# Sending the last 64 tokens of two batches in one transfer from interleaved partitions, and spreading the small row transfers that share the queue

## The chip, the cores and the metric

The kernel runs on one core of one Trainium2 chip. The metric is the time of one execution on the device in microseconds (us). Profiles are single executions; their span leaves out about 2 us of the time (427.3 us of span in the profiled run of the kernel before, 429.12 us of time).

## The reference

Sliding-window attention over 8 batches, 8 heads, 576 tokens and 64 channels per head feeds a spectral mixing layer:

```python
x = attention(q, k, v)                       # (8, 576, 512), window of 64 tokens
X = np.fft.rfft(x, axis=1)                   # 64 lowest modes are mixed
Y[:, :64] = complex einsum('bmd,mde->bme', X[:, :64], w_r + 1j * w_i)
y = np.fft.irfft(Y, n=576, axis=1)
u = x + y
return u + np.maximum(u @ w_ch, 0.0)         # (8, 576, 512) float32
```

The 64 pairs of 512x512 matrices w_r and w_i are most of the data read. What matters here is the end: u and the rectified product are formed tile by tile, and 9.44 MB of output leave the core.

## The kernel before

576 tokens are four tiles of 128 and a rest of 64. The rests of two batches share one tile, the *pair tile*: batch b on partitions 0 to 63, batch b+1 on 64 to 127. A whole-token tile pair (t, t+1) leaves as one transfer of 512 KB, 4 KB per partition; the pair tile leaves as two transfers of 64 partitions, 2 KB each. All of them are issued by SyncE. So are six small transfers, `send`, that copy eight late rows of a batch's spectrum (32 KB) to the tile that the matmuls of that batch read.

```python
def send(b):
    r0 = 2 * R + RL * (b - 2)
    nc.sync.dma_start(out=batch_tile(b)[128 - RL:].bitcast(FP32), in_=yl[r0:r0 + RL].bitcast(FP32))

def finish(n):
    b, t = seq[n]
    add(n, "Yb", True)                       # matmuls into PSUM
    ...
    nc.vector.tensor_tensor(out=ot[:, j], in0=ps, in1=x_sb[:, b, t, :], op=ALU.add)
    if t == NT - 1:                          # pair tile
        for i, queue in enumerate((nc.sync, nc.sync)):
            queue.dma_start(out=out[b + i, 128 * t:, :], in_=ot[64 * i:64 * i + 64, 0])
    ...
    elif j:                                  # two whole tiles
        nc.sync.dma_start(out=out[b, 128 * t - 128:128 * t + 128, :].rearrange("(p j) e -> p j e", j=2), in_=ot)

turn_of = {1: 3, 3: 4, 5: 5, 7: 6, 8: 7}     # after tile 1 send the rows of batch 3, ...
for n in range(NQ):                          # NQ = 36 tiles
    finish(n)
    if n in turn_of:                         # send(2), the first of the six, stands before this loop
        send(turn_of[n])
    ...                                      # rectify(n + 3), lay(n + 5)
```

The softmax here doesn't subtract the row's maximum and nothing guards it: scores larger than these inputs give would overflow.

Of the kernel before, what the change touches and what calls it, by code (L numbers as in the profile page):

```python
# [9 lines left out]
FP32 = mybir.dt.float32  # L10
FP32R = mybir.dt.float32r
BF16 = mybir.dt.bfloat16
# [14 lines left out]
def kernel(  # L27
# [10 lines left out]
    nc = tc.nc  # L38
    B, H, S, D = q.shape
# [532 lines left out]
    with ExitStack() as p2a:  # L572
# [4 lines left out]
        def channel(i):  # L577
            b, t = tiles[i]
            n = 1 if t == NT - 1 else 2
            psts = []  # L580
            for k in range(n):
                pst = ps_t.tile([128, NC, 128], BF16, name="pxt")
                for c in range(NC):
                    nc.tensor.transpose(out=pst[:, c, :], in_=x_sb[:, b, t + k, 128 * c:128 * c + 128],  # L584
                                        identity=ident_bf)
                psts.append(pst)
            for j in range(n):
                xT = xtp.tile([128, NC, 128], FP32R, name="xT")
                for k in range(n):
                    w = 128 // n  # L590
                    nc.vector.tensor_copy(out=xT[:, :, w * k:w * k + w], in_=view(psts[k], j, [[128, NC], [n, w]]))  # L591
                psz = ps_z.tile([128, DM], FP32, name="psz")
                for c in range(NC):
                    nc.tensor.matmul(out=psz, lhsT=xT[:, c, :], rhs=wch[:, c, :],  # L594
                                     start=(c == 0), stop=(c == NC - 1))
                nc.scalar.copy(out=channel_out(i + j), in_=psz)  # L596
            return n
# [3 lines left out]
        for m in range(L0 * MG):  # L601
# [13 lines left out]
            if m == Z_M - 2:  # L615

                with tc.tile_pool(name="tmpi", bufs=1, reuse_waits="tile") as tmp:
                    pcol = tmp.tile([128, 1], FP32, name="pcol")
                    nc.gpsimd.iota(pcol, pattern=[[0, 1]], base=0, channel_multiplier=1,
                                   allow_small_or_imprecise_dtypes=True)  # L620

                    SW = 128
                    pos = tmp.tile([128, SW + 64], FP32, name="pos")
                    nc.gpsimd.iota(pos[:, 0:SW], pattern=[[2, SW]], base=0, channel_multiplier=0,
                                   allow_small_or_imprecise_dtypes=True)
                    nc.gpsimd.iota(pos[:, SW:], pattern=[[1, 64]], base=512, channel_multiplier=0,
                                   allow_small_or_imprecise_dtypes=True)

                    def col(name):
                        return tmp.tile([128, 1], FP32, name=name)  # L630

                    def floor(d, p, name):
                        f = col(name)
                        nc.vector.tensor_scalar(out=f, in0=p, scalar1=1.0 / d, scalar2=0.5 / d - 0.5,
                                                op0=ALU.mult, op1=ALU.add)
                        nc.vector.tensor_scalar(out=f, in0=f, scalar1=MAGIC, scalar2=-MAGIC,
                                                op0=ALU.add, op1=ALU.add)
                        return f


                    for tab, row in ((trigI, pcol),):
                        fa, fb = floor(2 * MG, row, "fa"), floor(MG, row, "fb")

                        gcol, mcol = col("gcol"), col("mcol")
                        nc.vector.scalar_tensor_tensor(out=gcol, in0=fa, scalar=-2.0, in1=fb,
                                                       op0=ALU.mult, op1=ALU.add)
                        nc.vector.tensor_tensor(out=mcol, in0=fa, in1=fb, op=ALU.subtract)
                        nc.vector.scalar_tensor_tensor(out=mcol, in0=mcol, scalar=float(MG), in1=row,
                                                       op0=ALU.mult, op1=ALU.add)
                        for at, dg, dm in ((112 + ML, 1.0, -float(ML)), (112 + MG, -1.0, float(MG)),  # L650
                                           (112 + 2 * ML, -1.0, 0.0), (112 + 2 * ML + NLM, 1.0, -float(NLM))):
                            step = col("step")
                            nc.vector.tensor_single_scalar(out=step, in_=row, scalar=at - 0.5, op=ALU.is_ge)
                            nc.vector.scalar_tensor_tensor(out=gcol, in0=step, scalar=dg, in1=gcol,
                                                           op0=ALU.mult, op1=ALU.add)
                            if dm:
                                nc.vector.scalar_tensor_tensor(out=mcol, in0=step, scalar=dm, in1=mcol,
                                                               op0=ALU.mult, op1=ALU.add)
                        coef, coefs, coefc = col("coef"), col("coefs"), col("coefc")
                        nc.vector.tensor_single_scalar(out=coef, in_=mcol, scalar=0.0, op=ALU.is_equal)  # L660
                        nc.vector.tensor_scalar(out=coef, in0=coef, scalar1=-1.0 / S, scalar2=2.0 / S,
                                                op0=ALU.mult, op1=ALU.add)
                        nc.vector.tensor_tensor(out=coefs, in0=gcol, in1=coef, op=ALU.mult)
                        nc.vector.tensor_tensor(out=coefc, in0=coef, in1=coefs, op=ALU.subtract)
                        for i in range(NT):
                            n = SW if i < NT - 1 else 64
                            mt2 = tmp.tile([128, 2, SW], FP32, name="mti")[:, :, 0:n]
                            mt = mt2[:, 0, :]
                            nc.vector.tensor_scalar(out=mt, in0=pos[:, 0:SW] if n == SW else pos[:, SW:],
                                                    scalar1=float(256 * (i // 2) + i % 2) if n == SW else 0.0,  # L670
                                                    scalar2=mcol, op0=ALU.add, op1=ALU.mult)
                            tis = tmp.tile([128, SW], FP32, name="tis")[:, 0:n]
                            gen_trig(tmp, mt2, n, mt, tis, "i")
                            nc.vector.tensor_scalar(out=tis, in0=tis, scalar1=coefs, scalar2=None, op0=ALU.mult)
                            o = SW * i if n == SW else 576
                            nc.vector.scalar_tensor_tensor(out=tab[:, o:o + n], in0=mt, scalar=coefc, in1=tis,
                                                           op0=ALU.mult, op1=ALU.add)
                    nc.vector.tensor_scalar(out=view(trigI, 512, [[128, 2], [1, 64]]),
                                            in0=view(trigI, 0, [[64, 2], [1, 64]]), scalar1=0.0,
                                            scalar2=None, op0=ALU.mult)  # L680
                    nc.vector.tensor_scalar(out=view(YTl, R - RL, [[R, NC * B], [1, RL]]),
                                            in0=view(trigI, 0, [[RL, NC * B], [1, RL]]), scalar1=0.0,
                                            scalar2=None, op0=ALU.mult)
# [90 lines left out]
        for j in range(2):  # L774
            evac(x_sb[:, b, 2 * h + j, :], ps[j], j)

    spreads = [(b, h) for b in range(B) for h in range(2)]

    with tc.manual_schedule(engines={mybir.EngineType.PE}):
        for m in range(M0, ME):  # L780
            while len(spreads) > 2 * B * (ME - 1 - m) // (ME - M0):
                spread(*spreads.pop(0))
            if (m - M0) % 2 == 0 and (m - M0) // 2 < B // 2:
                b0 = m - M0
                mode(m, lambda: spectrum(b0))
# [48 lines left out]
    with tc.manual_schedule(engines={mybir.EngineType.PE, mybir.EngineType.Activation, mybir.EngineType.DVE,  # L834
# [20 lines left out]
        def add(n, what, stop):  # L855
            b, t = seq[n]
            for bb, r0, k in parts_of(b, t):
                tr = 128 * t + (64 - r0 if t == NT - 1 else 0)
                nc.tensor.matmul(out=tps[n], lhsT=trigI[:, tr:tr + 128], rhs=pair_tile(what, bb),  # L859
                                 start=False, stop=stop and r0 + k == 128, skip_group_check=True)  # L860

# [6 lines left out]
        def finish(n):  # L868
# [12 lines left out]
                return  # L881
            nc.vector.tensor_tensor(out=ot[:, j], in0=ps, in1=x_sb[:, b, t, :], op=ALU.add)  # L882
            if t == NT - 1:
                for i, queue in enumerate((nc.sync, nc.sync)):
                    queue.dma_start(out=out[b + i, 128 * t:, :], in_=ot[64 * i:64 * i + 64, 0])
            elif n == NQ - 2:
                nc.sync.dma_start(out=out[b, 128 * t:128 * t + 256, :].rearrange("(p j) e -> p j e", j=2)[:, 0],
                                  in_=ot[:, 0])
# [7 lines left out]
            if n == 2:  # L896
                nc.scalar.copy(out=yl[0:NR, 0], in_=psw[0:NR])
        send(2)
        turn_of = {1: 3, 3: 4, 5: 5, 7: 6, 8: 7}
        for n in range(NQ):  # L900
            finish(n)
            if n in turn_of:
# [39 lines left out]
```

## Time and profile before

| | |
|---|---|
| time, median of the first 3 runs | 429.73 us (429.59 to 430.24) |
| span of the profile | 427.3 us |
| weights stream, until the last weight matmul | 391.2 us |
| first DVE cast of the tail (it takes up the last weights' products) / last output add ends | 391.87 / 420.39 us |
| output leaves | 399 to about 426.1 us |

Three more lines say how the tail works. The first is from the page (busy time, share of the span, instructions of each engine), the others from the table of waits between 391 and 428 us (who waited for what: us in total, times, longest).

```profile
PE 322.1 (75%) x5179; PEld 230.8 (54%) x5186; DVE 176.1 (41%) x372; ACT 164.1 (38%) x290; POOL 89.4 (21%) x171
...
PEld pso L859 <- ACT pso L864: 1.7, 6, 0.4
DVE ot L882 <- PE pso L859: 1.1, 5, 0.3
```

The shares are averages over stages with different limits and say nothing of the tail. The waits do: in some 28 us of tail, PE's loads wait 1.7 us for ACT and DVE 1.1 us for PE. (A pair of names like `PEld pso L859 <- ACT pso L864` reads: the loads of line 859 waited for ScalarE's line 864.) The producers run at their pace, and what is left to win lies between the last add and the end.

### The profile page before, as it was taken

To read this page: it belongs to the slowest core of one execution; us is meant where nothing else is said; L and a number is where in the kernel's file an instruction comes from. 1 tells how busy PE (TensorE), PEld (TensorE's weight loads), DVE (VectorE), ACT (ScalarE), POOL (GpSimd) and SP (SyncE) were. 2 spreads that over 40 slices of the span, in tenths; PEclk is the share of its full clock that TensorE was granted. 3 is DMA by queue.
4 is the path that set the end of the run, shared out by engine and by line. 5 is a ranking of instruction groups with operands and counts; after the bars stand their busy time and mean duration, and the time that the engine had idled before them with its cause. 6 is when DMAs were issued, how large, how long until landed. Compare 5 with 4: busy or idle time off the path is not lost.

```text
span 427.3 us, 11629 instructions
## 1 busy us (share of the span) xinstructions
PE 322.1 (75%) x5179; PEld 230.8 (54%) x5186; DVE 176.1 (41%) x372; ACT 164.1 (38%) x290; POOL 89.4 (21%) x171
## 2 busy tenths in 40 slices
PE   6989998998998866422488877876367685498992
PEld 5755765765665566411367666654245452266781
DVE  5566765765764200306223332221113332141993
ACT  4585765866863221001022322222012221131991
POOL 7231231241112232211221221221111122100000
PEclk9999998999996655555588998899556965589997
DMA  7999999999999999999999999999999999993698
GB/s 142 212 213 213 213 212 213 214 211 214 214 213 213 214 213 261 214 214 213 213 213 215 213 212 214 214 214 213 212 215 213 214 213 214 214 214 68 219 351 333
DMA packets 28721, 92.16 MB, mean 216 GB/s; under 512 B 2896, under 2 KB 3152, under 8 KB 28672
## 3 DMA queue, kind: packets, MB, share of 16 engines
q0 software_dynamic: 25344, 81.80, 96.1%
q1 hardware_dynamic: 3184, 9.50, 6.0%
q8 instruction: 40, 0.66, 0.6%
q10 hardware_dynamic: 144, 0.13, 0.1%
q14 instruction: 9, 0.07, 0.0%
HBM read 162.53 MB, written 9.44 MB: 402 GB/s over the span
## 4 chain that ended last, share of the span: by engine, by line
DMA 51%; PE 32%; DVE 8%; issue 4%; ACT 2%; POOL 1%; DVEq 0%; POOLq 0%
DMA wt<-in_moe_w_i_dram 45%; PE pso L316 7%; PE pst L218 6%; DMA wy<-in_moe_w_i_dram 4%; PE pso L859 4%; PE psv L235 3%; DVE x_sb L324 3%; PE pss L372 3%; PE pss L272 2%; DMA wt<-in_moe_w_r_dram 2%; PE psx L338 2%; PE pss L291 2%; DVE vT L59 2%; PE psw L709 1%; DVE ot L882 1%
## 5 line engine op out<-in xcount | busy, mean ns | idle before, releaser
L563 PE MATMUL psy<-XQ,wt 128*128 128x16 bf16 x1616 | 61.4, 191 | 72.8 <-DMA wt<-in_moe_w_i_dram 37.6
L563 PEld LDWEIGHTS <-wt 128*128 128x128 bf16 x1616 | 53.2, 103 | 87.5 <-DMA wt<-in_moe_w_i_dram 42.4
L591 DVE CAST xT<-pxt 128x256 fp32r<-128x256 bf16 (+1 forms) x68 | 26.1, 434 | 61.8 <-PE pxt L584 39.4
L115 POOL DMA_DIRECT2D wt<-in_moe_w_r_dram x54 | 29.0, 537 | 87.8 <-DMA wt<-in_moe_w_r_dram 42.2
L596 ACT CAST Z<-psz 128x512 fp32r<-128x512 f32 x36 | 21.1, 586 | 66.9 <-PE psz L594 66.6
L115 POOL DMA_DIRECT2D wt<-in_moe_w_i_dram x52 | 27.9, 536 | 84.7 <-DMA wt<-in_moe_w_i_dram 53.7
L594 PE MATMUL psz<-wch,xT 128*128 128x512 f32 x144 | 45.3, 457 | 0.0
L297 ACT ACTIVATE et<-pss 128x512 bf16<-128x512 f32 x72 | 39.2, 599 | 13.2 <-PE pss L291 13.2
L316 PE MATMUL pso<-vt,et 128*64 128x65 bf16 (+1 forms) x576 | 34.3, 210 | 5.2 <-DVE x_sb L324 5.1
L316 PEld LDWEIGHTS <-et 128*64 128x64 bf16 (+1 forms) x576 | 23.9, 114 | 17.3 <-issue 9.8
L594 PEld LDWEIGHTS psz<-wch,xT 128*128 128x128 f32 x144 | 29.2, 217 | 5.8 <-ACT Z L596 0.4
L324 DVE TENSOR_TENSOR x_sb<-pso,rcp 128x640 bf16<-128x640 f32 x32 | 26.3, 822 | 0.9
L859 PE MATMUL pso<-Y,trigI 128*128 128x512 f32 x80 | 23.1, 402 | 0.1
L59 DVE CAST YT<-psy 128x256 fp32r<-128x256 f32 x6 | 2.5, 423 | 49.4 <-PE psy L563 49.4
L882 DVE TENSOR_TENSOR ot<-pso,x_sb 128x512 f32<-128x512 f32 x35 | 22.2, 685 | 1.5 <-PE pso L859 1.1
L59 DVE CAST x_sb<-psj 128x512 bf16<-128x512 f32 x16 | 11.0, 688 | 27.2 <-PE psj L771 27.1
L58 ACT CAST YT<-psy 128x256 fp32r<-128x256 f32 x6 | 2.2, 373 | 50.7 <-DVE YT L59 50.7
L272 PE MATMUL pss<-band,ident_bf 64*64 64x512 bf16 x136 | 20.5, 414 | 1.5 <-ACT et L297 1.5
L59 DVE COPY vT<-pst 128x768 bf16<-128x768 bf16 x16 | 15.3, 957 | 13.0 <-PE pst L218 13.0
L58 ACT CAST x_sb<-psj 128x512 bf16<-128x512 f32 x16 | 9.4, 586 | 26.9 <-PE psj L771 26.9
L864 ACT ACTIVATE pso<-pso 128x512 f32<-128x512 f32 x36 | 19.1, 597 | 0.0
L859 PEld LDWEIGHTS pso<-Y,trigI 128*128 128x128 f32 x80 | 14.5, 188 | 5.5 <-ACT pso L864 1.7
(158 smaller groups left out, 496.3 us busy)
## 6 DMA issues: line engine op xcount, KB each, us to landing
wt<-in_moe_w_r_dram POOLq DMA_DIRECT2D x54, 512.0 KB, 19.1
wt<-in_moe_w_i_dram POOLq DMA_DIRECT2D x52, 512.0 KB, 19.1
out_dram<-ot SPq DMA_DIRECT2D x15, 512.0 KB, 4.2
rk<-in_k_dram POOLq DMA_DIRECT2D x8, 576.0 KB, 9.0
rq<-in_q_dram POOLq DMA_DIRECT2D x8, 576.0 KB, 12.9
rv<-in_v_dram POOLq DMA_DIRECT2D x8, 576.0 KB, 11.9
wy<-in_moe_w_r_dram POOLq DMA_DIRECT2D x3, 512.0 KB, 16.9
wy<-in_moe_w_i_dram POOLq DMA_DIRECT2D x3, 512.0 KB, 19.1
```

The costliest lines, as they stand in the source:

```text
L59: return nc.vector.tensor_copy(out=o, in_=i)
L115: nc.gpsimd.dma_start(out=wt, in_=src[m].rearrange("(p c) e -> p c e", c=NC))
L218: nc.tensor.transpose(out=ps[64 * hh:64 * hh + 64, c, :], in_=src[:, hh, (c0 + c) * D:(c0 + c + 1) * D], identity=ident_bf)
L272: nc.tensor.matmul(out=pss[(2 * w + hh) % 3][64 * half:64 * half + 64, :], lhsT=ident_bf[pp, pp], rhs=view(band[pp], 128 * half, [[0, WIN ...
L297: nc.scalar.activation(out=et[:, hh, :], in_=pss[(2 * w + hh) % 3], func=ACT_F.Exp, scale=EX_SCALE)
L316: nc.tensor.matmul(out=pso[po, hh, (i // 2) * VW:(i // 2) * VW + D + 1], lhsT=et[pk, hh, col:col + 64], rhs=vt[pk, 1 - f % 2, 2 * hh + g / ...
L324: nc.vector.tensor_tensor(out=view(x_sb, b * NT * DM + g * D, [[4 * D, 2], [DM, NT], [1, D]]), in0=view(pso, 0, [[512, 2], [VW, NT], [1, D]]),
L563: nc.tensor.matmul(out=psy[:, m % MG, e, :], lhsT=w[:, c, 128 * e:128 * e + 128], rhs=XQ[:, c, :, 1 - im:3 - im, m], start=(m % MG == im + ...
L591: nc.vector.tensor_copy(out=xT[:, :, w * k:w * k + w], in_=view(psts[k], j, [[128, NC], [n, w]]))
L594: nc.tensor.matmul(out=psz, lhsT=xT[:, c, :], rhs=wch[:, c, :], start=(c == 0), stop=(c == NC - 1))
L859: nc.tensor.matmul(out=tps[n], lhsT=trigI[:, tr:tr + 128], rhs=pair_tile(what, bb), start=False, stop=stop and r0 + k == 128, skip_group_c ...
L882: nc.vector.tensor_tensor(out=ot[:, j], in0=ps, in1=x_sb[:, b, t, :], op=ALU.add)
```

## The change

The intent: the pair tile gets the two batches on alternate partitions (token s of batch b+i on partition 2s+i), so that one transfer over all 128 partitions can carry both; and the row transfers go out less densely. For this, a permutation matmul reorders each pair tile of x while weights still stream (four matmuls, and four copies of their results back into x, called evacuations), and the table of sines for the pair tile gets zeros at every second column instead of in halves.

```diff
+    def spread_pair(b):
+        psj = lo.tile([128, DM], FP32, name="psj", tag="s2")
+        nc.tensor.matmul(out=psj, lhsT=turn, rhs=x_sb[:, b, NT - 1, :], start=True, stop=True)
+        evac(x_sb[:, b, NT - 1, :], psj, b % 4 == 0)
...
+    turn = wl.enter_context(tc.tile_pool(name="turn", bufs=1)).tile([128, 128], BF16, name="turn")
+    nc.vector.tensor_copy(out=view(turn, 0, [[2, 64], [1, 2]]), in_=view(ident_bf, 0, [[1, 64], [64, 2]]))
...
-                tr = 128 * t + (64 - r0 if t == NT - 1 else 0)
+                tr = 128 * t + (t == NT - 1 and r0 == 0)
...
-                for i, queue in enumerate((nc.sync, nc.sync)):
-                    queue.dma_start(out=out[b + i, 128 * t:, :], in_=ot[64 * i:64 * i + 64, 0])
+                nc.sync.dma_start(out=out[b:b + 2, 128 * t:, :].rearrange("i s e -> s i e"), in_=ot[:, 0])
...
-        turn_of = {1: 3, 3: 4, 5: 5, 7: 6, 8: 7}
+        turn_of = {1: 3, 5: 4, 9: 5, 12: 6, 15: 7}
```

Cut: the strided writes of the sine table and the strided read in the cast of the pair tile for the channel product.

More of the change, by code (lines that the diff above doesn't have):

```diff
@@ L590, in channel @@
                     w = 128 // n
-                    nc.vector.tensor_copy(out=xT[:, :, w * k:w * k + w], in_=view(psts[k], j, [[128, NC], [n, w]]))
+                    nc.vector.tensor_copy(out=xT[:, :, w * k:w * k + w],
+                                          in_=view(psts[k], j, [[128, NC], [n, w]] if n > 1 else
+                                                   [[128, NC], [1, 64], [64, 2]]))
                 psz = ps_z.tile([128, DM], FP32, name="psz")
@@ L674 @@
                             nc.vector.tensor_scalar(out=tis, in0=tis, scalar1=coefs, scalar2=None, op0=ALU.mult)
-                            o = SW * i if n == SW else 576
-                            nc.vector.scalar_tensor_tensor(out=tab[:, o:o + n], in0=mt, scalar=coefc, in1=tis,
+                            o = SW * i if n == SW else 513
+                            nc.vector.scalar_tensor_tensor(out=view(tab, o, [[1 if n == SW else 2, n]]), in0=mt, scalar=coefc, in1=tis,
                                                            op0=ALU.mult, op1=ALU.add)
-                    nc.vector.tensor_scalar(out=view(trigI, 512, [[128, 2], [1, 64]]),
-                                            in0=view(trigI, 0, [[64, 2], [1, 64]]), scalar1=0.0,
+                    nc.vector.tensor_scalar(out=view(trigI, 512, [[2, 65]]),
+                                            in0=view(trigI, 0, [[1, 65]]), scalar1=0.0,
                                             scalar2=None, op0=ALU.mult)
@@ L775, in spread @@
             evac(x_sb[:, b, 2 * h + j, :], ps[j], j)
-    spreads = [(b, h) for b in range(B) for h in range(2)]
+    def spread_pair(b):
+        psj = lo.tile([128, DM], FP32, name="psj", tag="s2")
+        nc.tensor.matmul(out=psj, lhsT=turn, rhs=x_sb[:, b, NT - 1, :], start=True, stop=True)
+        evac(x_sb[:, b, NT - 1, :], psj, b % 4 == 0)
+    spreads = [(b, h) for b in range(B) for h in range(2 + (b % 2 == 0))]
+    turn = wl.enter_context(tc.tile_pool(name="turn", bufs=1)).tile([128, 128], BF16, name="turn")
+    nc.vector.tensor_copy(out=view(turn, 0, [[2, 64], [1, 2]]), in_=view(ident_bf, 0, [[1, 64], [64, 2]]))
     with tc.manual_schedule(engines={mybir.EngineType.PE}):
         for m in range(M0, ME):
-            while len(spreads) > 2 * B * (ME - 1 - m) // (ME - M0):
-                spread(*spreads.pop(0))
+            while len(spreads) > 5 * B // 2 * (ME - 1 - m) // (ME - M0):
+                b0, h = spreads.pop(0)
+                spread(b0, h) if h < 2 else spread_pair(b0)
             if (m - M0) % 2 == 0 and (m - M0) // 2 < B // 2:
```

## The prediction

> **What bounds the kernel now.** I read the page first, then the SyncE timeline and a table by windows of the last 30 us, then the waits of the tail. The page shows two regimes.
>
> ```profile
> DMA  7999999999999999999999999999999999993698
> q1 hardware_dynamic: 3184, 9.50, 6.0%
> out_dram<-ot SPq DMA_DIRECT2D x15, 512.0 KB, 4.2
> out_dram<-ot SPq DMA_DIRECT2D x9, 128.0 KB, 3.5
> ```
>
> In slices 2 to 36 the DMA engines are full: the weights stream in, and nothing that the compute engines do there matters unless the stream starves. The chain of waits agrees (51% of it is DMA, 45% the one weight line). Slice 37 ends the stream; the last weights are consumed at 391.2 us. Then all output, 9.44 MB, leaves in some 28 us. The change acts on this tail. The eight 128 KB transfers of the second out_dram group that come from L885 are the pair tiles (a ninth is the last half tile).
>
> What ends last in the tail? The windows (columns: window, length, busy time of PE, PEld, DVE, ACT, POOL, then PE clock, DMA share, GB/s):
>
> ```profile
> 399.00:401.00 2.00, 2.00 (x10) 1.60 (x9) 1.71 (x4) 2.00 (x6) 0.00 (x0) 1.00 0.98 320
> 401.00:403.00 2.00, 2.00 (x10) 1.52 (x10) 1.91 (x5) 2.00 (x6) 0.00 (x0) 1.00 0.89 340
> 403.00:405.00 2.00, 2.00 (x11) 1.61 (x10) 1.80 (x3) 2.00 (x6) 0.00 (x0) 1.00 0.94 375
> 405.00:407.00 2.00, 2.00 (x10) 1.65 (x9) 1.90 (x4) 2.00 (x5) 0.00 (x0) 1.00 0.76 227
> 407.00:409.00 2.00, 2.00 (x10) 1.59 (x10) 2.00 (x5) 2.00 (x5) 0.00 (x0) 1.00 0.87 348
> 409.00:411.00 2.00, 2.00 (x10) 1.61 (x9) 1.80 (x4) 2.00 (x5) 0.00 (x0) 1.00 0.98 327
> 411.00:413.00 2.00, 2.00 (x10) 1.62 (x9) 1.90 (x4) 2.00 (x5) 0.00 (x0) 1.00 1.01 402
> 413.00:415.00 2.00, 2.00 (x11) 1.59 (x10) 1.68 (x4) 1.98 (x5) 0.00 (x0) 1.00 1.04 420
> 415.00:417.00 2.00, 2.00 (x10) 1.65 (x9) 1.99 (x4) 2.00 (x5) 0.00 (x0) 1.00 0.97 338
> 417.00:419.00 2.00, 2.00 (x7) 0.94 (x6) 2.00 (x4) 1.55 (x4) 0.00 (x0) 1.00 1.02 408
> 419.00:421.00 2.00, 0.10 (x1) 0.00 (x0) 1.39 (x4) 0.00 (x0) 0.00 (x0) 1.00 0.99 352
> ```
>
> From 411 us on the DMA engines are full; before that they have gaps (0.76 to 0.94). PE and ACT are full as well, and hand tiles to DVE. So producer and DMA run at nearly the same pace, and the DMA side ends later:
>
> ```profile
> 413.30 6.43 DVE L882 TENSOR_TENSOR ot<-pso,x_sb 128x512 f32<-128x512 f32 x10 [0.21 <-PE pso L859]
> 419.65 0.74 DVE L879 TENSOR_TENSOR ot<-pso,x_sb 128x256 f32<-128x256 f32 x2
> 419.13 2.17 SPq L890 DMA_DIRECT2D out_dram<-ot  x3
> 421.39 1.12 SPq L887 DMA_DIRECT2D out_dram<-ot  x1
> 422.60 1.17 SPq L880 DMA_DIRECT2D out_dram<-ot  x1
> ```
>
> DVE is done at 420.4, but SyncE issues the last half tile only at 422.6 (its data were ready at about 420.1) and the queue drains until about 426.1; the span ends at 427.3. The backlog was built up before 411 us, in the gaps. They stand where SyncE is late:
>
> ```profile
> 404.02 1.42 SPq L885 DMA_DIRECT2D out_dram<-ot  x2
> 405.55 0.68 SPq L848 DMA_DIRECT2D Y<-yl  x1
> 406.33 0.85 SPq L890 DMA_DIRECT2D out_dram<-ot  x2
> 407.27 2.16 SPq L885 DMA_DIRECT2D out_dram<-ot  x2
> ```
>
> The first two tiles sent by the 406.33 row were added by 403.6 (DVE row 400.33, five adds of 0.65): SyncE is 2.7 us late there, having issued six small row transfers (L848) of 0.66 us each between the large ones.
>
> **What the Trainium skill says.** "SBUF — State Buffer", section "Door 1: The DMA port swizzle": partitions 0 to 63 reach only 8 of the 16 ports, so a transfer of 64 partitions gets about half the rate of one of 128. The trace agrees in direction: the stretch of the first pair, 405.6 to 406.8, has 242 GB/s at share 0.81, and that of the second, 410.0 to 410.8, has 261 at 0.93, against 402 at 1.01 between pairs. Per busy engine that is 0.70 to 0.75 of the full rate; not half[...]. "DMA: Bandwidth & Descriptors", section "Rules for kernel authors", advises one 128-partition transfer in place of two on disjoint halves, which is this change. The same page, section "Issuing engines are not separate DMA queues", says the sequencer's time to initiate a DMA is usually small relative to the DMA. Here it is not: an L885 issue has a median of 1.03 us, and its 128 KB need 0.32 us at 408 GB/s.
>
> **The change, part by part.**
>
> 1. Preparing the interleaved pairs: four more matmuls with a permutation (L771's form: 0.41 us each), four evacuations (0.59 us on ACT, 0.69 on DVE) and one copy of 128x128; the cast of the pair tiles reads with a stride (today 0.69 us, four of them). That is about 5 us of work in pieces of under 1 us, spread over 205 to 370 us, where the DMA share is 1.06 and PE is busy 6.6 of 12 us (window 352 to 364). Transfers of weights take 19 us from issue to landing, so the queue is deep; a delay of under 1 us on PE does not empty it. Cost on the path: 0, at most 0.2 us. The zeros and sines of the table are rewritten with a stride, also there: 0. Matmuls, ACT and DVE work in the tail stay the same in number and size.
>
> 2. Pair output in one DMA: 8 issues become 4. Packets stay 2 KB and bytes stay 1.05 MB. SyncE saves about four times 1.0 us. On the DMA engines: full-rate windows (411-413, 413-415, 417-419, 421-423: 402, 420, 408, 405) average 409 GB/s. The two windows with late pairs lose (409-338)x2 + (409-352)x2 = 256 KB, 0.63 us at 409. The same for the two early pairs gives 1.26 us. The last half tile, also of 2 KB pieces, makes me expect that not all of it comes back, and part of the early loss would be hidden by waiting for data; I take 0.8 us.
>
> 3. Row transfers spread out: five of the six L848 issues stand after tiles 1, 5, 9, 12, 15 instead of 1, 3, 5, 7, 8. From 399 to 411 the windows carried (320+340+375+227+348+327)x2 = 3.87 MB; at 409 it would be 4.91. The deficit of 1.03 MB is 2.5 us. Of it 0.63 is the early pairs (counted above) and 0.44 the start (window 399-401, where the order of transfers barely changes); some 1.45 us is left for lateness of SyncE. Counting SyncE's work in the new order with the old durations, it reaches each tile within 0.8 us of its add: 397.9 (tiles 0-1), 399.6, 400.1, 401.7, the pair at 402.3, 403.8, 405.1, second pair at 406.2. DVE supplies 256 KB per 0.66 us, 397 GB/s, a bit below the full rate, so some gaps stay. I take 1.1 us of the 1.45. The rows are needed much later than they are sent: those of batch 7 go after tile 15 (about 407 us) for tile 27, whose matmul is near 413.
>
> Sum: 0 + 0.8 + 1.1 = 1.9 us. Upper bound: last add at 420.4, plus an issue of about 0.4 to 1.2 us, plus about 1.7 us to land on a short queue (4.1 us for the last ACT transfer, less 2.4 us of backlog in front of it), gives 423; so at most 3.1 us. 429.7 - 1.9 = 427.8 us.
>
> **The rivals.** (a) *The queue is full anyway:* if the engines' own speed bounds the whole tail (shares of 0.98 at 399-401 and 409-411 with only 320 to 327 GB/s speak for slow packets rather than late ones), spreading the rows gives nothing and the gain is only the pair part, 0.3 to 0.8 us: about 429.2. Against it: shares of 0.76 and 0.87 between 405 and 409. (b) *The producer takes over:* PE and ACT are full until 419, so past the bound above nothing is to be had; at best 426.6. (c) *A late row transfer holds up PE:* a matmul waits for rows of batch 3 or 4. The first comes unchanged after tile 1; the second moves only from tile 3 to tile 5, about 6 us ahead of its use. It would cost 1 us if wrong; I give it 5%. (d) *The interleaved transfer is itself slow:* neighbouring partitions go to rows of two batches, and if its descriptors are spread over the ports no better than the halves were, the 0.8 us is lost and 1 us remains: 428.7. (e) *The weight stream starves* through the extra work at 300 to 370 us: small, it would add up to 0.5 us.
>
> **Range and chances.** The main case is 427.8; the bound of the producer puts the low end at 426.7, rivals (a) and (d) the high end at 429.2. Faster by over 2% would need 8.6 us, almost three times the bound: 0.01. Slower by over 2% would need a stall that nothing shows: 0.01. Within 2%: 0.98.
>
> **What would show it.** Right: windows from 401 to 411 at shares over 0.95 and 370 GB/s or more; windows with pairs near 390; SyncE's last issue within 1.5 us of the last add; the end of the DMA near 424; the last add unchanged within 0.3 us of 29.2 us after the last weight matmul; four pair issues, each under 1.2 us. Wrong: pair windows still at 340 (rival d); gaps filled but rate unchanged (rival a); PE waiting for a Y<-yl transfer (rival c); last weight matmul later than 391.5 (rival e).

## The result, and the profile after

The kernel after took 428.31 us (median of 4 runs, 428.14 to 428.46), the kernel before 429.81 us beside it: 1.5 us less. The ratio is 0.9964, 95% interval 0.9947 to 0.9981. A ratio here is the mean time of one kernel's fast runs over that of the other's in the same rounds, so it is not quite the ratio of the medians. By the bound of 2% it is the same; the interval says that it is a little faster.

On the page of the kernel after, and in its DMA view, these lines answer to the first ones in the prediction (queue, packets, MB, share of 16 engines' span; then transfers with size and time to landing; the last line is the four pairs and one whole tile):

```profile
q1 hardware_dynamic: 3120, 9.50, 5.8%
...
out_dram<-ot SPq DMA_DIRECT2D x15, 512.0 KB, 4.4
...
out_dram<-ot SPq DMA_DIRECT2D x5, 256.0 KB, 3.8
```

The bytes are the same and the packets took 5.8% of 426.7 us instead of 6.0% of 427.3 us, 24.7 for 25.6 us per engine: 0.9 us of DMA work is gone. The trace's packet records say where: the 640 packets of 2 KB took 103 ns on average before and 85 ns after, (103 - 85) x 640 / 16 = 0.7 us. The windows of the tail (window, length, busy time of PE, PEld, DVE, ACT, POOL, clock, DMA share, GB/s):

```profile
399.00:401.00 2.00, 2.00 (x10) 1.50 (x9) 1.72 (x4) 2.00 (x5) 0.00 (x0) 1.00 0.89 287
401.00:403.00 2.00, 2.00 (x10) 1.51 (x9) 1.90 (x4) 2.00 (x5) 0.00 (x0) 1.00 0.86 328
403.00:405.00 2.00, 2.00 (x10) 1.65 (x10) 1.80 (x4) 2.00 (x5) 0.00 (x0) 1.00 1.00 383
405.00:407.00 2.00, 2.00 (x11) 1.59 (x10) 1.89 (x4) 2.00 (x5) 0.00 (x0) 1.00 0.99 389
407.00:409.00 2.00, 2.00 (x10) 1.60 (x9) 2.00 (x4) 2.00 (x5) 0.00 (x0) 1.00 0.98 388
409.00:411.00 2.00, 2.00 (x10) 1.63 (x10) 1.80 (x4) 2.00 (x5) 0.00 (x0) 1.00 0.96 380
...
415.00:417.00 2.00, 2.00 (x11) 1.60 (x10) 1.93 (x4) 1.98 (x5) 0.00 (x0) 1.00 1.02 398
417.00:419.00 2.00, 2.00 (x9) 1.11 (x7) 2.00 (x5) 1.91 (x4) 0.00 (x0) 1.00 1.03 399
419.00:421.00 2.00, 0.47 (x1) 0.15 (x1) 1.76 (x4) 0.00 (x0) 0.00 (x0) 1.00 1.01 401
```

The gap at 405 to 409 us is closed, and no window with a pair falls to 340 any more. The first 4 us have changed little: the tail starts 0.35 us later in this profile, and in windows moved by as much (399.35 to 403.35 us) they carry 320 and 363 GB/s, against 320 and 340 before. The end, from DVE's timeline and from SyncE's (start and duration in us, engine, line, operation):

```profile
420.02 0.75 DVE L890 TENSOR_TENSOR ot<-pso,x_sb 128x256 f32<-128x256 f32 x2
```

```profile
417.08 2.79 SPq L900 DMA_DIRECT2D out_dram<-ot  x3
420.13 0.94 SPq L897 DMA_DIRECT2D out_dram<-ot  x1
421.17 1.12 SPq L891 DMA_DIRECT2D out_dram<-ot  x1
```

SyncE starts its last issue 0.4 us after the last add; it was 2.2 us before. The last add is where it was: 28.55 us after the first DVE cast of the tail, 28.52 before. In this profile that cast came at 392.22 us instead of 391.87. Is that the price of the reordering? No: kernels below without it have 392.13 and 392.19, and one profile of the kernel after had 394.38, in a run of 430.38 us. The start of the tail varies from run to run, so the span from that first cast to the end is the better measure of the tail in a profile: 35.4 us before, 34.5 after.

### The profile page after: what moved, and what is told of

Its sections match the earlier page's. It is cut to its first block, busy times and chain, and to the rows that moved or that the text cites. A ratio compares the mean times of both kernels' runs of the same rounds, so it can differ in the third digit from the quotient of the medians.

```text
span 426.7 us, 11631 instructions
## 1 busy us (share of the span) xinstructions
PE 320.8 (75%) x5179; PEld 229.7 (54%) x5190; DVE 178.0 (42%) x375; ACT 165.0 (39%) x292; POOL 89.2 (21%) x171
## 4 chain that ended last, share of the span: by engine, by line
DMA 49%; PE 36%; DVE 8%; issue 4%; ACT 2%; POOL 1%; DVEq 0%; POOLq 0%
DMA wt<-in_moe_w_i_dram 22%; DMA wt<-in_moe_w_r_dram 18%; DMA wy<-in_moe_w_r_dram 9%; PE pso L316 7%; PE pst L218 6%; PE pso L870 4%; PE psv L235 3%; PE psy L563 3%; DVE x_sb L324 3%; PE pss L372 3%; PE pss L272 2%; PE psx L338 2%; PE pss L291 2%; DVE vT L59 2%; PE psz L596 1%
## 5 line engine op out<-in xcount | busy, mean ns | idle before, releaser
L563 PE MATMUL psy<-XQ,wt 128*128 128x16 bf16 x1616 | 61.3, 191 | 73.7 <-DMA wt<-in_moe_w_i_dram 34.7
L115 POOL DMA_DIRECT2D wt<-in_moe_w_r_dram x54 | 28.9, 536 | 87.3 <-DMA wt<-in_moe_w_r_dram 42.1
L596 PE MATMUL psz<-wch,xT 128*128 128x512 f32 x144 | 46.3, 465 | 0.0
L59 DVE CAST x_sb<-psj 128x512 bf16<-128x512 f32 x18 | 12.3, 689 | 26.3 <-PE psj L773 23.4
L58 ACT CAST x_sb<-psj 128x512 bf16<-128x512 f32 x18 | 10.5, 585 | 25.7 <-PE psj L773 25.7
```

What stands on the lines that cost most here:

```text
L59: return nc.vector.tensor_copy(out=o, in_=i)
L115: nc.gpsimd.dma_start(out=wt, in_=src[m].rearrange("(p c) e -> p c e", c=NC))
L563: nc.tensor.matmul(out=psy[:, m % MG, e, :], lhsT=w[:, c, 128 * e:128 * e + 128], rhs=XQ[:, c, :, 1 - im:3 - im, m], start=(m % MG == im + ...
L596: nc.tensor.matmul(out=psz, lhsT=xT[:, c, :], rhs=wch[:, c, :], start=(c == 0), stop=(c == NC - 1))
```

## The experiments

All ran 5 rounds beside the kernel before, and all results are correct. "Tail" is the span's end less the first DVE cast of the tail; "to last add" is the end of the last add less that cast; both in us, one profile each. The kernel after has a tail of 34.5 us in one profile and 34.2 in another, so differences of 0.3 us in that column say nothing. The runs stand on several chips; each was timed beside the kernel before, whose medians there are 429.77 to 430.06 us. Differences of under 0.5 us between two runs of this table are near the noise.

| run | median us (before beside it) | ratio, 95% interval | to last add | tail |
|---|---|---|---|---|
| before | | | 28.5 | 35.4 |
| e0_after, the kernel after again | 428.47 (429.77) | 0.9963, 0.9938 to 0.9989 | 28.5 | 34.2 |
| a_pairs, pair part alone | 428.82 (429.85) | 0.9978, 0.9966 to 0.9990 | 28.5 | 34.8 |
| b_spread, spreading alone | 430.03 (429.85) | 1.0009, 0.9996 to 1.0022 | 29.2 | 35.3 |
| h_earlier, milder spreading alone | 429.62 (429.77) | 0.9991, 0.9968 to 1.0014 | 28.6 | 35.3 |
| d_two, interleaved, two transfers | 429.20 (429.85) | 0.9995, 0.9978 to 1.0012 | 28.9 | 34.7 |
| c_one, halves, one transfer | 446.30 (429.85) | 1.0383, 1.0370 to 1.0397 | 40.1 | 52.5 |
| k_tiny, after + 8 tiny transfers | 429.70 (429.91) | 1.0001, 0.9980 to 1.0021 | 28.5 | 35.5 |
| f2_pool_before, rows by GpSimd | 429.78 (429.77) | 0.9989, 0.9967 to 1.0011 | 29.5 | 35.4 |
| f_pool, after + rows by GpSimd | 428.57 (429.77) | 0.9966, 0.9943 to 0.9989 | 29.8 | 34.7 |
| g_hybrid, after + 4 rows by GpSimd | 429.00 (429.91) | 0.9980, 0.9960 to 1.0001 | 29.6 | 34.5 |
| j_s3, after, first send later | 428.84 (429.91) | 0.9970, 0.9953 to 0.9987 | 29.1 | 34.8 |
| g2_gated, after + 4 gated rows | 428.88 (430.06) | 0.9970, 0.9950 to 0.9990 | 28.8 | 35.2 |

Theory at the start: both parts count, the pair transfers because each half reached half the ports, the spreading because SyncE was late. Rivals: one of the two parts is all of it.

**a_pairs: the pair part without the spreading.**

```diff
-        turn_of = {1: 3, 5: 4, 9: 5, 12: 6, 15: 7}    # from the kernel after
+        turn_of = {1: 3, 3: 4, 5: 5, 7: 6, 8: 7}
```

> The kernel after with the row transfers back at their old places (after tiles 1, 3, 5, 7, 8); pairs interleaved, one transfer each. Theory T (both parts count: full port reach in the pair transfers, and SyncE no longer late between 401 and 411 us): about 0.8 of the gain stays, 429.0 to 429.3 us against 429.8 before, windows with pairs near 390 GB/s but gaps between 401 and 411 us. Rival R1 (the pair part is all of it): 428.3, as the kernel after. Rival R2 (the spreading is all of it): 429.8.

Measured: 428.82 us, 1.0 us under before; a bit better than the theory's 429.0. One gap stays where the dense row transfers stand:

```profile
405.00:407.00 2.00, 2.00 (x11) 1.59 (x10) 1.90 (x4) 2.00 (x5) 0.00 (x0) 1.00 0.80 296
407.00:409.00 2.00, 2.00 (x10) 1.60 (x9) 2.00 (x4) 2.00 (x5) 0.00 (x0) 1.00 0.99 380
```

So rival R2 falls, and the pairs alone give two thirds of the gain. Against rival R1 the evidence is thinner: the intervals of a_pairs (0.9966 to 0.9990) and of the kernel after (0.9947 to 0.9981) overlap, but all five runs of a_pairs (428.74 to 429.12) lie above eight of the ten of the kernel after (428.12 to 428.57), and the gap at 405 us closes only in the latter.

**b_spread: the spreading without the pair part.**

```diff
-        turn_of = {1: 3, 3: 4, 5: 5, 7: 6, 8: 7}      # from the kernel before
+        turn_of = {1: 3, 5: 4, 9: 5, 12: 6, 15: 7}
```

> The kernel before with only the row transfers moved to the new places; pairs on halves, two transfers each. Theory T: 428.8 to 429.2 us; the 2 KB pair stretches stay at 240 to 300 GB/s. Rival R1 (the pair part is all): 429.8. Rival R2 (the spreading is all): 428.3.

Measured: 430.03 us, nothing gained. My theory fails here. The table of waits and three windows of its tail show why:

```profile
DVE ot L882 <- PE pso L859: 1.8, 5, 0.9
...
PEld pso L859 <- DMA Y<-yl: 0.8, 1, 0.8
```

```profile
411.00:413.00 2.00, 1.83 (x8) 1.12 (x6) 1.90 (x4) 2.00 (x5) 0.00 (x0) 1.00 0.95 348
...
415.00:417.00 2.00, 2.00 (x10) 1.65 (x9) 1.90 (x4) 2.00 (x5) 0.00 (x0) 1.00 0.96 334
...
419.00:421.00 2.00, 1.03 (x3) 0.37 (x2) 2.00 (x5) 0.48 (x1) 0.00 (x0) 1.00 1.00 344
```

PE waits 0.8 us for a row transfer, DVE then waits 0.9 us, and the last add comes 0.7 us later (29.2). The late windows with pairs are at 334 and 344 GB/s, as before. SyncE's timelines tell which rows were late; first this kernel, then the kernel after:

```profile
407.49 1.77 SPq L885 DMA_DIRECT2D out_dram<-ot  x2
409.34 0.53 SPq L890 DMA_DIRECT2D out_dram<-ot  x1
409.98 0.69 SPq L848 DMA_DIRECT2D Y<-yl  x1
```

```profile
406.94 1.12 SPq L895 DMA_DIRECT2D out_dram<-ot  x1
408.16 0.55 SPq L900 DMA_DIRECT2D out_dram<-ot  x1
408.81 0.65 SPq L859 DMA_DIRECT2D Y<-yl  x1
```

The same `send` of batch 7, after the same tile 15, starts at 409.98 us with two transfers per pair and at 408.81 with one. By the semaphore records of the traces the rows land 3.2 and 3.3 us later, at 413.21 and 412.14 us. PE's load that reads them starts at 413.25 us in b_spread, 0.8 us late; in the kernel after it starts at 412.55, and nothing waits. The same places are safe only with the other half of the change.

**h_earlier: a milder spreading alone, with the last rows after tile 11.**

```diff
-        turn_of = {1: 3, 3: 4, 5: 5, 7: 6, 8: 7}      # from the kernel before
+        turn_of = {1: 3, 5: 4, 7: 5, 9: 6, 11: 7}
```

> The kernel before with the row transfers spread a little less: after tiles 1, 5, 7, 9, 11. Theory L (the spreading alone gained nothing because the last rows, sent behind a full queue at 410 us, came late and held PE up): no wait of PE for a row transfer, last add at 29.0 to 29.2 us after the first cast of the tail, and 429.2 to 429.6 us. Rival N (the spreading is worth nothing while pairs take two transfers): 429.8 as before, with no PE wait.

Measured: no wait of PE for rows, the last add at 28.56 us, and 429.62 us: 0.15 us under before, with an interval that includes no change. It is on the edge of what theory L expected and says that this spreading is worth little while pairs take two transfers, even when nothing waits. It does not clear SyncE's queue at the gap, though: in its timeline two row transfers, at 405.32 and 406.58 us, still stand there. The gaps remain:

```profile
405.00:407.00 2.00, 2.00 (x11) 1.60 (x10) 1.89 (x4) 2.00 (x5) 0.00 (x0) 1.00 0.77 254
407.00:409.00 2.00, 2.00 (x10) 1.58 (x9) 2.00 (x4) 2.00 (x5) 0.00 (x0) 1.00 0.94 340
409.00:411.00 2.00, 2.00 (x10) 1.65 (x10) 1.80 (x4) 2.00 (x5) 0.00 (x0) 1.00 0.92 304
```

**d_two: interleaved pairs, but two transfers, one per batch.** It keeps eight issues and gives each transfer 64 partitions two apart.

```diff
-                nc.sync.dma_start(out=out[b:b + 2, 128 * t:, :].rearrange("i s e -> s i e"), in_=ot[:, 0])
+                for i in range(2):
+                    nc.sync.dma_start(out=out[b + i, 128 * t:, :], in_=ot[i::2, 0])
```

> The kernel after with each interleaved pair sent in two transfers, one per batch, each from 64 partitions two apart. It keeps the number of issues of the kernel before (8) and gives each transfer all 16 ports. Theory P (the ports make the pair part): pair stretches at 380 GB/s or more and 428.3 to 428.7 us. Rival Q (the number of issues makes it): pair stretches as slow as before, 429.0 or more.

Measured: 429.20 us, in between. (One of the six fast runs took 431.63 us, which lifts the mean in the ratio; the others lie between 428.85 and 429.48.) Compare its windows, shown after a line of its waits, with those of b_spread, whose transfers stand at the same places:

```profile
PEld pso L870 <- DMA Y<-yl: 0.5, 1, 0.5
```

```profile
415.00:417.00 2.00, 2.00 (x10) 1.61 (x9) 1.89 (x4) 1.98 (x5) 0.00 (x0) 1.00 0.99 384
...
419.00:421.00 2.00, 0.87 (x2) 0.25 (x2) 2.00 (x5) 0.31 (x1) 0.00 (x0) 1.00 1.02 395
```

Pair windows are back at 384 and 395 GB/s with the number of transfers unchanged: that is the layout over the partitions alone, and it is what the port formula in "SBUF — State Buffer", section "Door 1: The DMA port swizzle", says of every second partition (all values of the bits that choose the port occur). The packet records agree: 2 KB packets of 86 ns, against 104 in b_spread. PE's wait of 0.5 us for the last rows is still there, and with it the last add at 28.9 us. So theory P is right for the rate, while the time is the one that rival Q gave (429.0 or more): by medians 0.8 us (430.03 to 429.20) for the layout, another 0.7 to 0.9 us for one issue in place of two (to the kernel after, 428.31 and 428.47), PE's wait included.

**c_one: one transfer from halves.** Why interleave at all, if one transfer is wanted?

```diff
-                for i, queue in enumerate((nc.sync, nc.sync)):
-                    queue.dma_start(out=out[b + i, 128 * t:, :], in_=ot[64 * i:64 * i + 64, 0])
+                nc.sync.dma_start(out=out[b:b + 2, 128 * t:, :], in_=ot[:, 0])
```

with `turn_of` as in the kernel after.

> The layout of the kernel before (halves), but each pair in one transfer whose slowest dimension on the DRAM side is 2; row transfers at the new places. Theory K (the number of DMA engines of a transfer is the largest divisor up to 16 of both sides' slowest dimension, here 2, as the skill says): 128 packets of 2 KB go to two engines, 64 x 0.084 = 5.4 us or more for each pair while the others starve or wait in order; the tail gets 3 to 12 us longer, 431 to 441 us. Rival (one issue is all that is needed, the interleaving of partitions is not): 428.3, as the kernel after.

Measured: 446.30 us, 16 us slower; more than I had worked out, because row transfers queue behind the pairs and PE waits 8.1 us for them. While a pair is on its way:

```profile
411.00:413.00 2.00, 0.23 (x1) 0.24 (x2) 0.00 (x0) 0.00 (x0) 0.00 (x0) 1.00 0.16 62
...
421.00:423.00 2.00, 0.96 (x2) 0.83 (x3) 0.00 (x0) 0.13 (x1) 0.00 (x0) 0.50 0.13 53
```

A share of 0.13 to 0.16 of 16 engines is 2.1 to 2.6 engines. The page "DMA: Bandwidth & Descriptors", section "Why a DMA increments its semaphore by 16 and not by 1", says that the number of engines is the largest divisor up to 16 that both sides' slowest dimensions share; with 2 on one side that is two, and the profile agrees. The dimension of 64 that the interleaving puts first is what makes one transfer affordable.

**k_tiny: what do small transfers on the queue cost, apart from their bytes?**

```diff
+        tiny = yp.tile([8, 8, 16], FP32, name="tiny")
+        TINY = (17, 19, 21, 22, 24, 26, 27, 29)
...
+            if n in TINY:                    # in the kernel after, after send
+                nc.sync.dma_start(out=tiny[:, TINY.index(n), :], in_=yl[0:8, 0, 0:16].bitcast(FP32))
```

> The kernel after with eight tiny transfers (8 partitions of 64 bytes, to an unused tile) added on SyncE's queue after tiles 17, 19, 21, 22, 24, 26, 27, 29, where SyncE has slack. Theory D (the number of outstanding transfers is the limit): each tiny one takes a place in the queue until the data ahead of it have gone, so fewer bytes are in flight: DMA share under 0.95 between 411 and 421 us, output issues of about 1 us or more, 429.0 to 430.5 us. Rival B (bytes or packets are the limit): shares stay at 0.99 to 1.03, 428.3 to 428.6 us.

Measured: 429.70 us, 1.2 to 1.4 us over the kernel after: eight transfers of 512 bytes undo nearly the whole gain. (In its profile the tail starts 1.9 us later than in that of the kernel after; compare times from there.) Two windows and SyncE's timeline:

```profile
417.00:419.00 2.00, 2.00 (x10) 1.65 (x9) 1.99 (x4) 1.99 (x5) 0.00 (x0) 1.00 0.73 279
...
421.00:423.00 2.00, 0.33 (x1) 0.01 (x1) 1.62 (x4) 0.00 (x0) 0.00 (x0) 0.98 0.76 291
```

```profile
413.15 0.63 SPq L902 DMA_DIRECT2D out_dram<-ot  x1
413.83 0.64 SPq L917 DMA_DIRECT2D tiny<-yl  x1
414.56 0.79 SPq L902 DMA_DIRECT2D out_dram<-ot  x1
415.40 0.64 SPq L917 DMA_DIRECT2D tiny<-yl  x1
416.13 0.70 SPq L897 DMA_DIRECT2D out_dram<-ot  x1
```

Rival B falls: bytes are not what such a transfer costs, since its 64-byte packets took 10 ns each in the records. Theory D is not proved either. I had written that SyncE has slack there; it hasn't. A tiny issue takes 0.64 us, an output issue here up to 0.79, and SyncE is busy nearly without a break: it comes to this pair (L897) 22.0 us after the first cast of the tail, and to the same pair in the kernel after (412.30 us) 20.1 us after it. Whether the queue also limits how many transfers are outstanding stays open. Issues of the same 512 KB take from 0.33 to over 1 us, but by the semaphore records of the kernel after the short ones and the long ones alike find three to five transfers on their way. Either way, the number of transfers on SyncE's queue is the cost here.

**f2_pool_before and f_pool: the row transfers issued by GpSimd,** in the kernel before and in the kernel after:

```diff
-            nc.sync.dma_start(out=batch_tile(b)[128 - RL:].bitcast(FP32), in_=yl[r0:r0 + RL].bitcast(FP32))
+            nc.gpsimd.dma_start(out=batch_tile(b)[128 - RL:].bitcast(FP32), in_=yl[r0:r0 + RL].bitcast(FP32))
```

> The kernel before with the six row transfers issued by GpSimd instead of SyncE, which takes their 4 us of issue time off SyncE and their queueing behind the output. Theory S (SyncE lateness before 411 us is worth what I predicted): gaps between 401 and 407 us close and the time falls by 0.5 to 1.1 us, 428.8 to 429.3. Rival N (with two transfers per pair the queue has slack of its own): 429.7 to 429.9.

> The kernel after with the six row transfers issued by GpSimd instead of SyncE. Theory S (what is left of gaps from 399 to 403 us in the kernel after comes from SyncE issuing row transfers): windows 399 to 403 at 350 GB/s or more, 427.6 to 428.0 us. Rival W (the gaps come from the slow 4 KB packets of the row transfers themselves, about 1 us each[...]): windows from 399 to 403 still at 290 to 330 GB/s and 428.2 to 428.4 us.

Measured: 429.78 and 428.57 us: no gain over the kernels they are made from, so theory S is not borne out in either. The runs are not clean: GpSimd issues all six within 3.0 us, and PE waits for the first rows (1.1 us and 1.4 us), so the last add is 0.9 and 1.3 us later. For f_pool the windows from 401 to 405 us carry 211 and 318 GB/s. (Its tail starts 1.2 us later than that of the kernel after; at the same distance from the first cast, the first 4 us of output carry 227 and 336 GB/s against 320 and 363.) So these two runs do not tell what SyncE's time alone is worth.

**g_hybrid: two row transfers on SyncE, four by GpSimd,** and **g2_gated: the same, each of the four behind a one-element copy that makes it wait for an output tile.**

```diff
+            if b > 3:                        # g2_gated only, and turn_of = {1: 3, 7: 4, 10: 5, 13: 6, 15: 7}
+                nc.gpsimd.tensor_copy(out=gate[:, b:b + 1], in_=ots[0][0:1, 0, 0:1])
+            queue = nc.sync if b < 4 else nc.gpsimd
```

> The kernel after with the first two row transfers (batches 2, 3) on SyncE as before and the last four (batches 4 to 7) issued by GpSimd. If SyncE's queue lets only about three transfers be outstanding, whatever their size, then four small ones taken out of it let more bytes be in flight: SyncE issues of 0.33 to 0.6 us, DMA share from 401 to 411 us at 0.97 or more, no PE wait for rows, 427.8 to 428.2 us, under the kernel after. Rival (nothing left to gain there, the slow row packets themselves cost the time): 428.3 to 428.5.

> The kernel after with the row transfers of batches 4 to 7 issued by GpSimd, each behind a one-element GpSimd copy that reads the output tile just added (after tiles 7, 10, 13, 15), so that they do not crowd the first two. In the run where GpSimd issued them ungated the DMA share was near 1 from 405 us on and SyncE's output issues were mostly 0.33 to 0.6 us, but PE waited 1.4 us for the first rows. Theory: without that wait the last add is back at 28.5 us after the first cast of the tail, the span from that cast to the end shrinks by 0.3 to 0.7 us under the kernel after (34.5 us), and the time is 427.7 to 428.2 us. Rival (the row transfers cost the DMA engines the same from any queue): 428.3 to 428.6 us.

Measured: 429.00 and 428.88 us, both slightly over the kernel after. In g_hybrid PE again waits 1.4 us for rows. In g2_gated only 0.4 us of that is left, SyncE has four transfers less, and still nothing is won; while the last rows move, the DMA engines are full but slow:

```profile
409.00:411.00 2.00, 2.00 (x11) 1.60 (x10) 1.80 (x4) 1.98 (x5) 0.00 (x0) 1.00 0.99 329
```

This speaks for the rival of g2_gated, that the row transfers cost the DMA engines time from whichever queue they come: of the 16 packets of GpSimd's last two row transfers, from 408.6 us on, seven took over 0.3 us, up to 1.14, against 0.16 for a usual packet of 4 KB. It is not proved, since the time lies above the rival's range too and PE still waits.

**j_s3: the first of the spread row transfers after tile 3 instead of 1.**

```diff
-        turn_of = {1: 3, 5: 4, 9: 5, 12: 6, 15: 7}
+        turn_of = {3: 3, 5: 4, 9: 5, 12: 6, 15: 7}
```

> The kernel after with the row transfer of batch 3 sent after tile 3 instead of tile 1. If the gap at 399 to 401 us (share 0.89) comes from SyncE sending that small transfer ahead of tiles 2 and 3, it closes by about 0.2 us: 428.1. Rival (the first packets are slow anyway): 428.3 to 428.5. PE waits for those rows (needed near 404 us) would show as 0.3 us or more and make it slower than 428.5.

Measured: 428.84 us. PE waits 0.6 us for these rows (a wait that the kernel after does not have), and the last add is 0.6 us later. The window 399 to 401 us stays at 289 GB/s, which looks like the rival's sign, but fixed windows mislead here: the output has hardly begun at 399 us. Shorter windows show a slow stretch that moved with the transfer. The first line is from the kernel after, 8.5 us after its first cast of the tail; the second is the same place in j_s3, the third 1.5 us later there:

```profile
400.72:401.72 1.00, 1.00 (x6) 0.82 (x5) 1.00 (x2) 1.00 (x3) 0.00 (x0) 1.00 0.95 213
```

```profile
400.83:401.83 1.00, 1.00 (x6) 0.82 (x5) 1.00 (x2) 1.00 (x3) 0.00 (x0) 1.00 1.03 406
402.33:403.33 1.00, 1.00 (x6) 0.61 (x4) 1.00 (x2) 1.00 (x4) 0.00 (x0) 1.00 0.64 234
```

The kernel before has 213 GB/s at that place too. The share of 0.95 in the first line says that the engines were busy and not waiting for tiles. So this row transfer makes the stretch slow; sending it later moves the loss and does not remove it. By an estimate from these lines it is (409 - 213) x 1 us = 0.2 MB, or 0.5 us of the DMA engines.

**e0_after: the kernel after again, as reference.**

> The kernel after again, as the reference on this chip: 428.3 us, 1.5 us under before. The pairs alone gave 428.82 and the spreading alone 430.03, where PE waited 0.8 us for the last row transfer; so the spreading should be worth about 0.5 us beside single pair transfers.

Measured: 428.47 us, ratio 0.9963. No version here beats the kernel after; f_pool, at 428.57, is level with it. In the kernel after the last rows land 0.4 us before they are read.

## Why the prediction was right or wrong

The time was 0.5 us above the forecast and inside its range, and the class was right. The steps:

1. **Preparation costs nothing: right.** The tail starts at 392.2 us with it (kernel after, a_pairs, d_two at 392.3) and without it (392.13 in b_spread, 392.19 in h_earlier).
2. **Pair part, 0.8 us: right in mechanism and about in size.** Alone it gave 1.0 us by medians and 0.6 us of tail in the profiles. d_two shows that alternate partitions bring the windows with pairs from 334 and 344 to 384 and 395 GB/s, and c_one that a single transfer from halves is no way out. Rival (d) did not come true.
3. **Spreading, 1.1 us: the term that was mis-sized.** Beside the pair part it is worth 0.35 to 0.5 us (428.82 to 428.47 and 428.31); alone nothing (430.03, and 429.62 in the milder form). I had given to the row transfers all of the deficit before 411 us that was left after 0.63 us for the pairs and 0.44 us for the start. Windows laid at the same distance from the first cast of the tail (12 us from 399.0 in the kernel before, one profile each) show how that deficit against 409 GB/s divides: 1.03 MB before, 0.65 in a_pairs with the rows still at their old places, 0.49 in the kernel after. So in these windows the pairs closed 0.38 MB or 0.93 us instead of 0.63, and the spreading beside them 0.17 MB or 0.41 us instead of 1.1. Of the rest 0.27 MB lies in the first 4 us, where I had booked 0.18 MB as the start; j_s3 puts most of it down to a row transfer that is slow wherever it stands. Spreading alone (b_spread) closed 0.25 MB there and lost 0.14 MB again in the next 10 us, where PE waited for rows. Why the two half transfers cost more early than late is argued, not shown: SyncE has little time to spare there, and the first pair's issues took 1.84 us in b_spread, its one issue 0.65 us in the kernel after. The pair part was set too low and the spreading too high, so that the sum came near (1.9 forecast, 1.5 measured) is in part luck.
4. **The bound of 3.1 us** was not reached: the DMA engines stayed full to the end at about 400 GB/s, rather than idling for the last add. SyncE's last issue moved as expected, the end of the DMA did not reach 424; by the packet records it was 425.2 us.
5. **Rival (c), a late row transfer, got 5%.** In the kernel after, it does not occur. But I took the margin from the order of SyncE's issues alone, about 6 us for the last rows. In the kernel after they are sent at 408.81 us instead of 407, take 3.3 us to land, and come 0.4 us before the load that reads them. b_spread, d_two and j_s3 all ran into it with one small step, 0.5 to 0.8 us each.

What stays open: whether an issue on SyncE waits for a free place in the queue or only takes its own time; and why some row transfers are slow. In the slow stretch of the kernel after, from 400.8 us, seven packets of 4 KB take 0.8 to 1.1 us each in the packet records, against 0.16 us for a usual one; in j_s3 such packets stand from 402.2 us instead. I take them for those of the second row transfer. The four later transfers of the kernel after show none above 0.41 us.

## What to carry to other kernels

When output leaves at the pace of the DMA engines, count transfers on the issuing queue as well as bytes: merge halves into one transfer over all partitions, and choose the layout so that the merged transfer's slowest dimension still divides by 16. Compare windows of two profiles at the same distance from a common event, not at the same time of the clock. Before moving a small transfer later in a full queue, add the time until the issuing engine reaches it, and the time that it takes to land behind what is on its way; the wait comes back on the engine that reads it. Split a two-part change by experiment before believing how the gain divides: here one part was worth something only beside the other.

## What the Trainium skill lacked or had wrong

- "DMA: Bandwidth & Descriptors", section "Issuing engines are not separate DMA queues", calls the issue time usually small. Here SyncE needed at least 0.64 us for a transfer of 8 partitions even when it carried 512 bytes, and 0.33 to over 1 us for 512 KB; eight such tiny transfers cost 1.2 to 1.4 us. The page has one count of sequencer cycles per transfer instruction for the generations before trn3, in its part on trn3; I found no figure there for how the issue time depends on shape, nor for when an issue blocks.
- The same page's advice on two transfers from disjoint partition halves ("Don't bother", section "Rules for kernel authors") held, 1.0 us for four pairs. The obvious merge (2 x 64 rows on the DRAM side) falls to two engines, 16 us slower in c_one; the row "Use all 16 engines" of the same section warns of that, and the advice on halves does not point to it. What the page lacks is the way out taken here, alternate partitions for the two batches.
- No page that I read gives the packet times of a small SBUF-to-SBUF transfer beside a stream of output. In f_pool, where the rows' 48 packets of 4 KB are alone on GpSimd's queue, they took 0.16 to 1.19 us, 16 of them over 0.5 us; a usual one takes 0.16 us.
